# Masks ahead of a turn's gelus, paced weight rounding, the bounds check on ScalarE and interleaved first operands in a routing attention with an MLP

## The chip, the cores and the metric

The kernel runs on one core of a Trainium2 chip. The metric is the device time of one execution in microseconds (us). The engines of the core each work through an instruction stream of their own, in order: TensorE (PE in the profile, its weight loads PEld), VectorE (DVE), ScalarE (ACT), GpSimd (POOL), and SyncE (SP), which issues most of the DMAs. They wait for each other by semaphores.

## The reference

A masked attention, in which a query sees only the keys of its own cluster, is followed by an MLP with a quick gelu:

```python
# q, k, v: (B=4, H=8, S=768, D=64) float32; centroids: (8, 16, 64)
q_assign = argmax(q_n @ c_n)            # normalised vectors, 16 clusters
k_assign = argmax(k_n @ c_n)
mask = q_assign[:, :, :, None] == k_assign[:, :, None, :]
scores = where(mask, (q @ k.T) / 8, -1e9)
attn = exp(scores - max); attn /= attn.sum() + 1e-9
x = (attn @ v).transpose(0, 2, 1, 3).reshape(3072, 512)
h = x @ w_in                            # w_in (512, 2048), float64
g = h * (1 / (1 + exp(-1.702 * h)))
out = (g @ w_out).astype(float32)       # w_out (2048, 512), float64
```

Both MLP weights arrive as float64 and have to be brought to float32 on the chip.

## The kernel before

The 32 heads are handled as 16 pairs p of two heads each, and a pair as two groups g of 384 queries. A group consists of six units u, one for each 128 keys. Two units make a turn t, so there are 96 turns, 24 for each batch element. A half block is the 12 turns that give 384 rows of x for all eight heads.

**Attention.** For each unit `scores` runs the matmuls of both heads into a PSUM tile s (L344; there are two, each of two banks) and the exponential on ScalarE in place (L349). `mask` multiplies on VectorE by "query's code equals key's code" (L358, twice for each unit) and gives A; GpSimd adds the A of a group into sum (L368, five times for each group). `values` multiplies A by v on TensorE (L379) one turn later. `normalise` comes two turns after a group's last unit: a matmul with ones (L391), reciprocal (L394) and product (L396) on VectorE, and a bounds check there (L398) whose result is kept in sums. Its verdict is read near the end and would send the program to a general path.

**Preparing a pair.** `PREP` is a list of seven steps: four turns of q and k by transposes on TensorE (L254), each copied out of PSUM (L260 on ScalarE, L262 on VectorE for the first of the four); `prep_near` (L271, L277), the products with the centroids; `prep_assign` (L282 and five operations on VectorE from L288 on), the codes; `prep_spread` (L309, the conversion L314, and two DMAs L316, L318), which sends the queries' codes through DRAM to all partitions as qb. The wrapper `prep` also issues loads: v of the pair before step 0, and the next q or k behind steps 1 and 3. The pools of these loads have few buffers, so a load waits for what frees its buffer, and SP issues everything in order.

**Weights.** They come in 32 chunks of 512 KB. Rounding step i issues the load of chunk i + 2 (L145), splits chunk i (L158, L160 on VectorE, L162, L164 on ScalarE) and joins chunk i - 1 (L170, L173 on VectorE, product L176 on GpSimd). The tile raw has three buffers, the tile e two. The order of the chunks is w_in first; each four chunks serve four MLP chunks.

**MLP.** The half block's 28 chunks are queued by the normalise of its last group: 16 of `first` (L417, tanh L422 on ScalarE, gelu L424 on VectorE, which frees the PSUM bank) and 12 of `second` (L434, output L440, L441). In each turn the loop takes as many as are due, part ahead of the preparation steps and part at the end of the turn. They share three PSUM banks m with the preparation and with normalise.

**Order.** The schedule is written out by hand: the engines get their instructions in program order. One turn before is: scores, MLP chunks, preparation steps, rounding steps by

```python
round_to(int(t * 2 / 3 if t < TB / 2 else
             TB / 3 + (t - TB / 2) * 2.3) - 1)
```

then masks, values of the turn before, normalise, MLP chunks. TB is 24. `first` and `second` call round_to themselves, too, so that no chunk comes ahead of its weights.

Of the kernel before, what the change touches and what calls it, by code (L numbers as in the profile page):

```python
# [8 lines left out]
FP32 = mybir.dt.float32  # L9
BF16 = mybir.dt.bfloat16  # L10
I32 = mybir.dt.int32
# [27 lines left out]
def fast(  # L39
# [113 lines left out]
    def split_w(i):  # L153

        hi = w_raw[i][:, :, 1]
        w = w_chunks[i][0]
        e = wp.tile([P, WN], I32, name="e", bufs=2)
        nc.vector.tensor_scalar(out=e, in0=hi, scalar1=EXP, scalar2=None,  # L158
                                op0=ALU.bitwise_and)
        nc.vector.tensor_scalar(out=w.bitcast(I32), in0=hi, scalar1=0xFFFFF,  # L160
                                scalar2=None, op0=ALU.bitwise_and)
        nc.scalar.activation(out=e, in_=e, func=AF.Relu, scale=8.0,  # L162
                             bias=low[:, 0:1])
        nc.scalar.activation(out=w, in_=w.bitcast(I32), func=AF.Copy,  # L164
                             scale=2.0 ** -20, bias=1.0)
        w_pow[i] = e
# [12 lines left out]
    w_done = [0]  # L179

    def round_to(n):

        while w_done[0] <= min(n, NW):
            i = w_done[0]
            if i < NW:
                load_w(i + 2)
                split_w(i)
            if i:
                join_w(i - 1)
            w_done[0] += 1  # L190

# [19 lines left out]
                   allow_small_or_imprecise_dtypes=True)  # L211
    sums = const.tile([P, 2 * NPAIR], FP32, name="sums")

# [34 lines left out]
    def prep_turn(p, i):  # L248
# [9 lines left out]
        dst = T[p, w][:, h * HALF:(h + 1) * HALF]  # L258
        if h or w:
            nc.scalar.copy(dst, ps[:, 0:HALF])  # L260
        else:
            nc.vector.tensor_copy(out=dst, in_=ps[:, 0:HALF])  # L262

# [42 lines left out]
    def prep_spread(p):  # L306
# [6 lines left out]
        row = asg.tile([n, P], U8, name="row")  # L313
        nc.vector.tensor_copy(out=row, in_=ps[0:n, 0:P])  # L314
        line = dram.tile([n, P], U8, name="line")
# [70 lines left out]
    def normalise(g):  # L386
# [3 lines left out]
        for a in range(2):  # L390
# [6 lines left out]

        nc.vector.scalar_tensor_tensor(  # L398
            out=rec, in0=ps[:, 0:HALF], scalar=1.0, in1=rec, op0=ALU.mult,
            op1=ALU.max, accum_out=sums[:, g:g + 1])  # L400
        if g % HP == HP - 1:
# [54 lines left out]
    prep_at = {}  # L456
    for p in range(2, NPAIR):
        b, hp = divmod(p, HP)
        for i, step in enumerate(PREP):
            if b == 0:  # L460
                t = (hp - 2) * TG + i * TG // len(PREP)
            else:
                t = b * TB + (-20, -8, -2, 1)[hp] + i
            prep_at.setdefault(t, []).append((p, i))
# [12 lines left out]
    owed = 0.0  # L477
    for p in range(2):
        for i in range(len(PREP)):
            prep(p, i)  # L480
    for t in range(NT + 2):
        us = range(2 * t, 2 * t + 2) if t < NT else ()
        for u in us:
            scores(u)
        owed = owed + rate if ffn else 0.0
        n = min(int(owed), len(ffn))
# [3 lines left out]
        for p, i in prep_at.get(t, ()):  # L490
            prep(p, i)
        round_to(int(t * 2 / 3 if t < TB / 2 else
                     TB / 3 + (t - TB / 2) * 2.3) - 1)
        for u in us:
            mask(u)
        if 1 <= t <= NT:
            for u in range(2 * t - 2, 2 * t):
                values(u)
        if t >= 2 and (t - 2) % TG == TG - 1:
            normalise((t - 2) // TG)  # L500
        for _ in range(n // 2):
            ffn.popleft()()


    ok = const.tile([P, 2 * NPAIR], FP32, name="ok")
    nc.vector.tensor_scalar(out=ok, in0=sums, scalar1=LIMIT, scalar2=None,
                            op0=ALU.is_le)
    ok1 = const.tile([P, 1], FP32, name="ok1")
    nc.vector.tensor_reduce(out=ok1, in_=ok, axis=AX.X, op=ALU.min)
    ps = bank()  # L510
# [450 lines left out]
```

## Time and profile before

| | |
|---|---|
| median of 3 runs | 1183.4 us (1183.03 to 1183.71) |
| the profiled execution | 1185.81 us, span in the trace 1184.0 us |
| TensorE busy | 1090.9 us, 92% of the span |
| VectorE, GpSimd, ScalarE busy | 513.4, 334.5, 306.6 us |
| mean granted TensorE clock | 0.959 of full speed |
| bytes moved | 45.92 MB, 39 GB/s over the span |

The span is the time from the first to the last instruction in the trace. A share of busy time is a mean over stages that have different limits; the granted clock is that which the throttle allowed TensorE, full speed being 2.4 GHz and the level below it 1.2 GHz. In the names of the rows s, m, A, qb and so on are the tiles named above, and "<-" after the bracket's idle time names what ended it.

### The profile page before, as it was taken

To read this page: it belongs to the slowest core of one execution; us is meant where nothing else is said; L and a number is where in the kernel's file an instruction comes from. 1 tells how busy PE (TensorE), PEld (TensorE's weight loads), DVE (VectorE), ACT (ScalarE), POOL (GpSimd) and SP (SyncE) were. 2 spreads that over 40 slices of the span, in tenths; PEclk is the share of its full clock that TensorE was granted. 3 is DMA by queue.
4 is the path that set the end of the run, shared out by engine and by line. 5 is a ranking of instruction groups with operands and counts; after the bars stand their busy time and mean duration, and the time that the engine had idled before them with its cause. 6 is when DMAs were issued, how large, how long until landed. Compare 5 with 4: busy or idle time off the path is not lost. (4 is left out here: it accounts for less than half of the span.)

```text
span 1184.0 us, 10396 instructions
## 1 busy us (share of the span) xinstructions
PE 1090.9 (92%) x3842; PEld 495.7 (42%) x3842; DVE 513.4 (43%) x897; ACT 306.6 (26%) x505; POOL 334.5 (28%) x200
## 2 busy tenths in 40 slices
PE   5767767759999999999999999999999999999997
PEld 3322333323444444544445444544444434443553
DVE  3688564644355234443354225433355334441110
ACT  2434333331233113321233122321232122310110
POOL 0555433343133133323222223323233223330000
PEclk8887888878999999999999999999999999999999
DMA  7432232321111000001111000102000000000000
GB/s 184 121 87 60 75 99 84 101 73 45 43 47 34 9 16 23 14 14 52 49 37 31 9 25 14 27 1 65 10 8 7 9 19 1 1 9 18 1 9 20
DMA packets 65484, 45.92 MB, mean 39 GB/s; under 512 B 52112, under 2 KB 58256, under 8 KB 65424
## 3 DMA queue, kind: packets, MB, share of 16 engines
q1 hardware_dynamic: 65280, 45.12, 13.7%
q8 instruction: 33, 0.54, 0.2%
q14 instruction: 27, 0.22, 0.1%
q10 hardware_dynamic: 144, 0.03, 0.0%
HBM read 38.83 MB, written 6.32 MB: 38 GB/s over the span
## 5 line engine op out<-in xcount | busy, mean ns | idle before, releaser
L434 PE MATMUL m<-w_out,g 128*128 128x512 f32 x768 | 355.3, 610 | 14.9 <-POOL w_out L176 14.9
L417 PE MATMUL m<-x,w_in 128*128 128x384 f32 x1024 | 362.7, 503 | 1.4 <-DVE bad L515 1.2
L368 POOL TENSOR_TENSOR sum<-sum,A 128x768 f32<-128x768 f32 x128 | 231.6, 1810 | 356.6 <-DVE A L358 351.6
L358 DVE SCALAR_TENSOR_TENSOR A<-qb,code,s 128x384 f32<-128x384 uint8 x384 | 209.7, 607 | 132.7 <-ACT s L349 101.7
L417 PEld LDWEIGHTS m<-x,w_in 128*128 128x128 f32 x1024 | 190.4, 194 | 172.7 <-issue 42.1
L434 PEld LDWEIGHTS m<-w_out,g 128*128 128x128 f32 x768 | 141.1, 192 | 208.8 <-issue 182.3
L344 PE MATMUL s<-T,T 64*128 64x384 f32 x768 | 169.3, 554 | 49.5 <-DVE A L358 47.4
L349 ACT ACTIVATE s<-s 128x768 f32<-128x768 f32 x192 | 145.9, 794 | 239.8 <-PE s L344 239.8
L424 DVE SCALAR_TENSOR_TENSOR g<-g,m 128x384 f32<-128x384 f32 x128 | 70.8, 553 | 276.9 <-ACT g L422 276.9
L379 PE MATMUL o<-A,inv 128*64 128x384 f32 x768 | 150.6, 515 | 0.0
L422 ACT ACTIVATE g<-m 128x384 f32<-128x384 f32 x128 | 62.8, 491 | 307.7 <-PE m L417 307.7
L368 POOL TENSOR_TENSOR sum<-A 128x768 f32<-128x768 f32 x32 | 61.0, 1907 | 262.9 <-DVE A L358 188.8
L344 PEld LDWEIGHTS s<-T,T 64*128 64x128 f32 x768 | 70.3, 199 | 146.1 <-issue 99.0
L394 DVE RECIPROCAL short<-m 128x384 f32<-128x384 f32 x32 | 81.6, 2550 | 34.0 <-PE m L391 34.0
L379 PEld LDWEIGHTS o<-A,inv 128*64 128x64 f32 x768 | 47.9, 140 | 71.6 <-issue 69.9
L440 ACT ACTIVATE y<-m 128x512 f32<-128x512 f32 x24 | 14.3, 598 | 133.5 <-PE m L434 120.3
L260 ACT COPY T<-m 128x384 f32<-128x384 f32 x48 | 22.9, 479 | 56.8 <-PE m L254 56.1
L254 PE MATMUL m<-ident,in 128*128 128x128 f32 x192 | 35.7, 313 | 2.0 <-ACT T L260 1.1
L176 POOL TENSOR_TENSOR w_out<-w_out,e 128x512 f32<-128x512 f32 x16 | 20.6, 1289 | 58.2 <-DVE w_out L173 58.2
L162 ACT ACTIVATE e<-e,low 128x512 int32<-128x512 int32 x32 | 23.1, 721 | 49.1 <-DVE e L158 48.9
L288 DVE TENSOR_REDUCE best<-m 128x24 f32<-128x384 f32 x16 | 8.9, 555 | 61.6 <-PE m L282 61.6
L176 POOL TENSOR_TENSOR w_in<-w_in,e 128x512 f32<-128x512 f32 x16 | 20.3, 1267 | 53.8 <-DVE w_in L173 53.8
(56 smaller groups left out, 313.8 us busy)
## 6 DMA issues: line engine op xcount, KB each, us to landing
raw<-in_moe_w_in_dram SPq DMA_DIRECT2D x16, 512.0 KB, 4.0
raw<-in_moe_w_out_dram SPq DMA_DIRECT2D x16, 512.0 KB, 3.4
in<-in_q_dram SPq DMA_DIRECT2D x32, 192.0 KB, 3.9
in<-in_k_dram SPq DMA_DIRECT2D x32, 192.0 KB, 3.3
inv<-in_v_dram SPq DMA_DIRECT2D x16, 384.0 KB, 4.5
out_dram<-y SPq DMA_DIRECT2D x24, 256.0 KB, 2.0
qb<-line SPq DMA_DIRECT2D x16, 192.0 KB, 3.2
line<-row SPq DMA_DIRECT2D x16, 1.5 KB
```

What stands on the lines that cost most here:

```text
L176: nc.gpsimd.tensor_tensor(out=w, in0=w, in1=e.bitcast(FP32), op=ALU.mult)
L254: nc.tensor.transpose(out=ps[:, n * P:(n + 1) * P], in_=qk_in[p, w][:, h * NH + n].rearrange("p a d -> p (a d)"), identity=ident)
L344: nc.tensor.matmul(out=ps[:, a, 0:HALF], lhsT=T[p, 1][rows, kt * P:(kt + 1) * P], rhs=T[p, 0][rows, h * HALF:(h + 1) * HALF], start=True, ...
L349: nc.scalar.activation(out=s, in_=s, func=AF.Exp, scale=SCALE)
L358: nc.vector.scalar_tensor_tensor(out=A[:, a, :], in0=qcode[p][:, a, h * HALF:(h + 1) * HALF], scalar=code[p][:, kt % NH, 1, kt // NH, a:a ...
L368: nc.gpsimd.tensor_tensor(out=sum_of[g], in0=A_of[u - 1] if kt == 1 else sum_of[g], in1=A, op=ALU.add)
L379: nc.tensor.matmul(out=o_of[g][a * D:(a + 1) * D, 0:HALF], lhsT=v_in[p][:, a, kt, :], rhs=A[:, a, :], start=(kt == 0), stop=(kt == NJ - 1))
L394: nc.vector.reciprocal(out=rec, in_=ps[:, 0:HALF])
L417: nc.tensor.matmul(out=ps[:, 0:HALF], lhsT=w_in[:, c, f * P:(f + 1) * P], rhs=xT[c], start=(c == 0), stop=(c == NCH - 1))
L422: nc.scalar.activation(out=g, in_=ps[:, 0:HALF], func=AF.Tanh, scale=0.851)
L424: nc.vector.scalar_tensor_tensor(out=g, in0=g, scalar=1.0, in1=ps[:, 0:HALF], op0=ALU.add, op1=ALU.mult)
L434: nc.tensor.matmul(out=ps[:, 0:DM], lhsT=hs[f][:, n * P:(n + 1) * P], rhs=w_out[:, f, :], start=(f == 0), stop=(f == NF - 1))
```

## The change

Six edits go together.

1. The masks of a turn stand right behind its scores and one rounding step, ahead of the turn's first MLP chunks and preparation steps.
2. Rounding goes by the new `round_next`: one step in each turn, ahead of the masks, and from turn 12 on a second one behind normalise. round_to stays as a guard in the MLP chunks.
3. The tile e has three buffers.
4. The bounds check is two ScalarE copies that add up (L399): one of the sums of exponentials, one of their reciprocals. It leaves VectorE.
5. All copies of turned operands, and the conversion in prep_spread, are on ScalarE.
6. The second pair's four transposing steps stand ahead of the first pair's last step; its other three steps are in turns 0 and 1. The third and fourth pairs' steps go two to a turn, from turns 1 and 4 on.

The core of the diff:

```diff
-        e = wp.tile([P, WN], I32, name="e", bufs=2)
+        e = wp.tile([P, WN], I32, name="e")
...
+    def round_next():
+        i = w_done[0]
+        if i < NW:
+            load_w(i + 2)
+            split_w(i)
+        if 0 < i <= NW:
+            join_w(i - 1)
+        w_done[0] += 1
+
     def round_to(n):
-
         while w_done[0] <= min(n, NW):
-            i = w_done[0]
-            if i < NW:
-                load_w(i + 2)
-                split_w(i)
-            if i:
-                join_w(i - 1)
-            w_done[0] += 1
+            round_next()
...
-    sums = const.tile([P, 2 * NPAIR], FP32, name="sums")
+    sums = const.tile([P, 2, 2 * NPAIR], FP32, name="sums")
...
-        if h or w:
-            nc.scalar.copy(dst, ps[:, 0:HALF])
-        else:
-            nc.vector.tensor_copy(out=dst, in_=ps[:, 0:HALF])
+        nc.scalar.copy(dst, ps[:, 0:HALF])
...
-        nc.vector.tensor_copy(out=row, in_=ps[0:n, 0:P])
+        nc.scalar.copy(row, ps[0:n, 0:P])
...
-        nc.vector.scalar_tensor_tensor(
-            out=rec, in0=ps[:, 0:HALF], scalar=1.0, in1=rec, op0=ALU.mult,
-            op1=ALU.max, accum_out=sums[:, g:g + 1])
+        junk = short()
+        for i, t in enumerate((ps[:, 0:HALF], rec)):
+            nc.scalar.activation(out=junk, in_=t, func=AF.Copy,
+                                 accum_out=sums[:, i, g:g + 1])
...
-    for p in range(2, NPAIR):
+    for p in range(1, NPAIR):
         b, hp = divmod(p, HP)
-        for i, step in enumerate(PREP):
-            if b == 0:
-                t = (hp - 2) * TG + i * TG // len(PREP)
+        for i in range(4 if p == 1 else 0, len(PREP)):
+            if p == 1:
+                t = i - 4 - i // 6
+            elif b == 0:
+                t = (hp - 2) * TG + 1 + i // 2
             else:
                 t = b * TB + (-20, -8, -2, 1)[hp] + i
...
-    for p in range(2):
-        for i in range(len(PREP)):
-            prep(p, i)
+    for p, i in [(0, i) for i in range(6)] + [(1, i) for i in range(4)]:
+        prep(p, i)
+    prep(0, 6)
     for t in range(NT + 2):
         us = range(2 * t, 2 * t + 2) if t < NT else ()
         for u in us:
             scores(u)
+        round_next()
+        for u in us:
+            mask(u)
         owed = owed + rate if ffn else 0.0
...
         for p, i in prep_at.get(t, ()):
             prep(p, i)
-        round_to(int(t * 2 / 3 if t < TB / 2 else
-                     TB / 3 + (t - TB / 2) * 2.3) - 1)
-        for u in us:
-            mask(u)
         if 1 <= t <= NT:
             for u in range(2 * t - 2, 2 * t):
                 values(u)
         if t >= 2 and (t - 2) % TG == TG - 1:
             normalise((t - 2) // TG)
+        if t >= TB // 2:
+            round_next()
         for _ in range(n // 2):
             ffn.popleft()()
```

On VectorE in turn 14, the first with MLP chunks, before: a gelu of that turn, two rounding steps (L158, L160 split one chunk, L170, L173 join the chunk before it), the masks A, and the gelu of the turn's second chunk.

```order
L424 SCALAR_TENSOR_TENSOR g_866<-g_866,m_861 128x384
L158 TENSOR_SCALAR e_871<-raw_813 128x512
L160 TENSOR_SCALAR w_in_106<-raw_813 128x512
L170 SCALAR_TENSOR_TENSOR e_825<-raw_781,e_825 128x512
L173 SCALAR_TENSOR_TENSOR w_in_106<-raw_781,w_in_106 128x512
L158 TENSOR_SCALAR e_881<-raw_823 128x512
L160 TENSOR_SCALAR w_in_106<-raw_823 128x512
L170 SCALAR_TENSOR_TENSOR e_871<-raw_813,e_871 128x512
L173 SCALAR_TENSOR_TENSOR w_in_106<-raw_813,w_in_106 128x512
L358 SCALAR_TENSOR_TENSOR A_889<-qb_205,code_195,s_853 128x384 x2
L358 SCALAR_TENSOR_TENSOR A_893<-qb_205,code_195,s_857 128x384 x2
L424 SCALAR_TENSOR_TENSOR g_906<-g_906,m_901 128x384
```

The same place now, from the end of turn 14's masks to the start of turn 15's:

```order
L357 SCALAR_TENSOR_TENSOR A_943<-qb_235,code_195,s_925 128x384 x2
L424 SCALAR_TENSOR_TENSOR g_952<-g_952,m_947 128x384
L158 TENSOR_SCALAR e_961<-raw_911 128x512
L160 TENSOR_SCALAR w_out_107<-raw_911 128x512
L170 SCALAR_TENSOR_TENSOR e_931<-raw_879,e_931 128x512
L173 SCALAR_TENSOR_TENSOR w_out_107<-raw_879,w_out_107 128x512
L424 SCALAR_TENSOR_TENSOR g_974<-g_974,m_969 128x384
L158 TENSOR_SCALAR e_987<-raw_929 128x512
L160 TENSOR_SCALAR w_out_107<-raw_929 128x512
L170 SCALAR_TENSOR_TENSOR e_961<-raw_911,e_961 128x512
L173 SCALAR_TENSOR_TENSOR w_out_107<-raw_911,w_out_107 128x512
L357 SCALAR_TENSOR_TENSOR A_995<-qb_312,code_302,s_977 128x384 x2
```

Each gelu is now followed by one step, and the masks of turn 14 are ahead of both; those of turn 15 have one step and no gelu of their own turn ahead of them.

On TensorE at the start, before: behind the first pair's spread (L309) come the second pair's transposes (L254), near (L271), assignment (L282) and spread, and then the first scores (L344).

```order
L309 MATMUL m<-ident_h,qc 12x128
L254 MATMUL m<-ident,in 128x128 x12
L271 MATMUL m<-T_209,cT 32x384 x2
L271 MATMUL m<-T_223,cT 32x384 x2
L282 MATMUL m<-ident,short 128x128 x3
L309 LDWEIGHTS qc
L309 MATMUL m<-ident_h,qc 12x128
L344 MATMUL s<-T_151,T_165 128x384 x4
```

The same place now, where lines are one to two lower or higher by the edits (L281 is the first pair's assignment, L256 the transposes, L308 the spread, L343 the scores, L270 near):

```order
L281 MATMUL m<-ident,short 128x128 x3
L256 MATMUL m<-ident,in 128x128 x12
L308 LDWEIGHTS qc
L308 MATMUL m<-ident_h,qc 12x128
L343 MATMUL s<-T_151,T_165 128x384 x4
L270 MATMUL m<-T_201,cT 32x384 x2
L270 MATMUL m<-T_215,cT 32x384 x2
```

The second pair's transposes stand ahead of the first pair's spread, and its near matmuls behind the first scores instead of ahead of them.

On ScalarE in turn 16, where before no check stood, now two chunks' tanh, a copy of turned operands, the two check passes (L399, the second reads the reciprocal), the split's two operations, a tanh and the next turn's exponentials:

```order
L422 ACTIVATE g<-m 128x384 x2
L261 COPY T_1079<-m 128x384
L399 ACTIVATE short,sums<-m 128x384
L399 ACTIVATE short,sums<-short 128x384
L162 ACTIVATE e<-e,low 128x512
L164 ACTIVATE w_out<-w_out 128x512
L422 ACTIVATE g<-m 128x384
L348 ACTIVATE s<-s 128x2x384 x2
```

The check passes are ahead of the turn's last tanh and of the next turn's exponentials on this engine.

## Rows read from the trace of the kernel before

**Rows 1.** View: busy time of each engine by stage (PE, PEld, DVE, ACT, POOL), then PE clock, DMA share, GB/s.

```profile
23.46:123.53 100.07, 70.18 (x305) 28.29 (x305) 72.94 (x127) 40.76 (x64) 50.79 (x30) 0.81 0.35 94
123.53:316.26 192.73, 151.54 (x471) 66.19 (x471) 101.88 (x183) 58.80 (x97) 70.69 (x46) 0.87 0.26 75
449.05:578.74 129.69, 129.63 (x474) 59.68 (x472) 56.80 (x92) 31.98 (x53) 39.38 (x22) 1.00 0.10 27
449.05:531.30 82.25, 82.19 (x314) 39.49 (x312) 40.15 (x67) 22.87 (x39) 24.92 (x14) 1.00 0.06 15
```

**Rows 2.** View: who waited for whom, 123.53 to 316.26: us in total, times, longest.

```profile
PE s L344 <- DVE A L358: 30.9, 8, 6.2
...
PE m L434 <- POOL w_out L176: 14.9, 5, 3.4
```

**Rows 3.** View: order of time on VectorE in one turn: start, duration, line, idle before.

```profile
144.05 0.56 DVE L424 SCALAR_TENSOR_TENSOR g<-g,m 128x384 f32<-128x384 f32 x1 [5.30 <-ACT g L422]
...
147.87 0.43 DVE L158 TENSOR_SCALAR e<-raw 128x512 int32<-128x512 int32 x1 [1.38 <-POOL w_in L176]
...
149.75 2.18 DVE L358 SCALAR_TENSOR_TENSOR A<-qb,code,s 128x384 f32<-128x384 uint8 x4
```

**Rows 4.** View: order of time on TensorE, the next turn's scores.

```profile
151.03 2.70 PE L344 MATMUL s<-T,T 64*128 64x384 f32 x8 [3.31 <-DVE A L358]
```

**Rows 5.** View: order of time at the start, several engines.

```profile
15.01 0.27 PE L309 MATMUL m<-ident_h,qc 128*12 128x128 bf16 x1 [2.63 <-DVE qc L302]
...
16.91 0.35 SPq L318 DMA_DIRECT2D qb<-line  x1
...
23.46 2.93 PE L344 MATMUL s<-T,T 64*128 64x384 f32 x8
...
27.73 2.18 DVE L358 SCALAR_TENSOR_TENSOR A<-qb,code,s 128x384 f32<-128x384 uint8 x4
```

**Rows 6.** View: DMA issues of the first 30 us: KB each, median us to landing.

```profile
qb<-line SPq DMA_DIRECT2D x2, 192.0 KB, 4.2
...
raw<-in_moe_w_in_dram SPq DMA_DIRECT2D x2, 512.0 KB, 6.7
```

**Rows 7.** View: groups by line on VectorE, 23.46 to 123.53: busy, mean ns, idle before.

```profile
L394 DVE RECIPROCAL short<-m 128x384 f32<-128x384 f32 x3 | 7.7, 2555 | 1.7 <-PE m L391 1.7
...
L262 DVE COPY T<-m 128x384 f32<-128x384 f32 x3 | 1.7, 558 | 9.8 <-PE m L254 9.8
...
L288 DVE TENSOR_REDUCE best<-m 128x24 f32<-128x384 f32 x3 | 1.7, 556 | 6.2 <-PE m L282 6.2
...
L314 DVE CAST row<-m 12x128 uint8<-12x128 bf16 x4 | 1.1, 279 | 3.4 <-PE m L309 3.4
```

**Rows 8.** View: order of time on VectorE and GpSimd, 63 to 72 us.

```profile
63.30 0.40 DVE L158 TENSOR_SCALAR e<-raw 128x512 int32<-128x512 int32 x1
...
65.17 2.17 DVE L358 SCALAR_TENSOR_TENSOR A<-qb,code,s 128x384 f32<-128x384 uint8 x4
...
65.32 1.27 POOL L176 TENSOR_TENSOR w_in<-w_in,e 128x512 f32<-128x512 f32 x1 [6.06 <-DVE w_in L173]
...
66.55 3.76 POOL L368 TENSOR_TENSOR sum<-sum,A 128x768 f32<-128x768 f32 x2
...
67.27 1.37 DVE L158 TENSOR_SCALAR e<-raw 128x512 int32<-128x512 int32 x1
...
68.56 2.04 DVE L160 TENSOR_SCALAR w_in<-raw 128x512 int32<-128x512 int32 x1
...
71.72 2.18 DVE L358 SCALAR_TENSOR_TENSOR A<-qb,code,s 128x384 f32<-128x384 uint8 x4
```

**Rows 9.** View: groups by line, whole span: busy us, mean ns, idle before.

```profile
L260 ACT COPY T<-m 128x384 f32<-128x384 f32 x48 | 22.9, 479 | 56.8 <-PE m L254 56.1
...
L396 DVE TENSOR_TENSOR x<-x,short 128x384 f32<-128x384 f32 x32 | 22.0, 688 | 1.2
...
L398 DVE SCALAR_TENSOR_TENSOR short<-m,short 128x384 f32<-128x384 f32 x32 | 17.8, 557 | 1.1
```

More of the change, by code (lines that the diff above doesn't have):

```diff
@@ L500, in fast @@
             normalise((t - 2) // TG)
+        if t >= TB // 2:
+            round_next()
         for _ in range(n // 2):
             ffn.popleft()()
-    ok = const.tile([P, 2 * NPAIR], FP32, name="ok")
+    ok = const.tile([P, 2, 2 * NPAIR], FP32, name="ok")
     nc.vector.tensor_scalar(out=ok, in0=sums, scalar1=LIMIT, scalar2=None,
@@ L508, in fast @@
     ok1 = const.tile([P, 1], FP32, name="ok1")
-    nc.vector.tensor_reduce(out=ok1, in_=ok, axis=AX.X, op=ALU.min)
+    nc.vector.tensor_reduce(out=ok1, in_=ok, axis=AX.XY, op=ALU.min)
     ps = bank()
```

## The prediction

> **What bounds the kernel now.** I read the busy time by stages first. The cuts are starts of turns, and a turn start is the moment at which TensorE begins a turn's score matmuls. Counting those, turn 0 begins at 23.46, turn 14 at 123.53, turn 26 at 316.26, turn 38 at 449.05 and turn 50 at 578.74. The MLP chunks of a half block run in the twelve turns that start two turns after its attention: those of the first half block in turns 14 to 25.
>
> The reader is to see in [rows 1] that the same kind of work takes two very different times. Turns 38 to 49 take 129.7 us, TensorE is busy for 129.6 of them and its granted clock is 1.00. Turns 14 to 25 hold the same matmuls (24 turns is the period of the schedule) and take 192.7 us, with TensorE busy 151.5, its clock at 0.87 and VectorE busy 101.9. So 63.0 us are lost in turns 14 to 25, part as idle time and part as matmuls at the lower of the two clock levels after the idle. From turn 26 on nothing is to be had: TensorE is the bound. Turns 0 to 13 carry no MLP work; there VectorE is the busiest engine, 72.9 of 100.1 us.
>
> The waits of turns 14 to 25 say who holds TensorE up [rows 2]: 30.9 us in 8 waits of the score matmul for VectorE's masks (a score bank comes free only when its mask has read it), and 14.9 us for output weights that GpSimd has not yet joined. The order of time of one such turn shows why the masks are late. VectorE sits 5.30 us in front of a gelu, whose tanh is not there yet, and only after it come two rounding steps, with 1.38 us of waiting for GpSimd's product between them (the two-buffer tile e), and then the masks [rows 3]. The masks end, and TensorE starts the next scores 3.31 us after it had run out of work, the first of them at the slow level: 2.70 us [rows 4].
>
> **The change, part by part.**
>
> *Start.* Scores of turn 0 begin at 23.46 because TensorE turns the second pair, brings it through its assignment and waits for VectorE there; the first masks start at 27.73 [rows 5]. Afterwards the second pair's twelve transposes run while VectorE assigns the first pair, its later steps follow in turns 0 and 1. What is late next is the first pair's spread code. Now its matmul ran at 15.01, its broadcast was issued at 16.91 and took 4.2 us to land [rows 5, 6], so it was there at 21.1. In the new order that matmul stands behind the twelve transposes, its copy behind four copies on ScalarE (0.48 us each [rows 9]), and its DMAs on SP behind one load of v and two pairs of loads of k and q that wait for those transposes. I add 1 us: masks at 22.1 instead of 27.73, minus 5.6 us. Bounds: minus 6.6 without that delay, 0 if the second pair's operands arrive late (a landing of 6.7 us was seen in this stretch [rows 6]).
>
> *Turns 0 to 13.* VectorE is the engine that has to get through. A step there costs 1.87 us where GpSimd is quiet (63.30 to the masks at 65.17) and 4.45 where it follows the masks at once and runs into GpSimd's two sums (67.27 to 71.72) [rows 8]. In turns 0 to 13 the steps up to the last masks grow from ten to fifteen: 5 x 1.87 = 9.4. The second pair's assignment moves in: four operations like the reduction of 0.556 and a small one, 2.4. Away go three bounds checks (0.557 and a short read, 1.8), three copies (1.7) and four conversions (1.1) [rows 7, 9]. Collisions: now the pattern of [rows 8] occurs twice in the stage; afterwards a step stands directly in front of the masks of each turn, with nothing between it and the masks before in turns 2, 5, 8 and 11, where GpSimd has two sums to do: 2 more, 2 x 2.58 = 5.2. Together 72.9 + 12.4 = 85.3 busy. Idle time was 27.1 us; the 9.8 in front of the copies and 3.4 in front of the conversions [rows 7] go, as both leave VectorE, and so do waits behind the e buffer like that in [rows 3], some 3 us, since it gets a third one. I keep the other 11. That makes 96.3 us against 100.1, minus 3.7. Bounds: minus 14 with no idle time left; plus 24 if every step collides (11 x 2.58 more).
>
> The Trainium skill, page "SBUF — State Buffer", section "Who interferes with whom", says that VectorE and GpSimd share one port pair as an exclusive lock: whichever starts first holds it for its whole instruction and the other blocks. The trace agrees: 1.37 and 2.04 us beside running sums where 0.40 is the quiet time [rows 8]. By that rule, applied to all four VectorE instructions of a step, this change moves more steps beside sums, and the sum would be that of the second rival below, 1162 us.
>
> *Turns 14 to 25.* Masks now follow one rounding step and stand ahead of the turn's gelus, the second step stands behind the first gelus, and by turn 14 sixteen instead of ten steps are issued, so that input weights are complete before the first chunk and output weights one or more turns ahead of their use. What VectorE has to do in turns 14 to 21 (the last with two steps): eight times four masks 17.4, sixteen steps 29.9, sixteen gelus of 0.56 9.0, two normalisations (2.56 and 0.69) 6.5, one assignment 2.4: 65.2 us, against 82.25 us that TensorE needs for the same eight turns at full clock [rows 1]. Waits for GpSimd: 16 x 2.58 = 41 at most. I take two full collisions (the short turns with two sums) and a wait for one product of 1.27 in each turn, 15 us: 80 us, just under TensorE's time. So TensorE is the bound, with little room: at the start of turn 14 VectorE still has a normalisation and two steps (7 to 8 us) ahead of the masks, which costs TensorE about 2 us, and uneven turns about 3. I take 129.7 + 5 = 134.7 instead of 192.7, minus 58.0. Bounds: 129.7 (minus 63), and 152 if every step collides (106 of VectorE's time against 82).
>
> *Costed at nothing.* The bounds check on ScalarE: two passes like the copy of 0.48 for each of 32 groups, 31 us on an engine that is busy 32 of 129.7 us [rows 1, 9]. The second pass waits for the reciprocal of 2.56 us, and tanh and the next turn's exponentials queue behind it; the cover is that TensorE has a turn's scores and a chunk to do before it needs a bank of theirs. From turn 26 on order alone changes under a saturated TensorE. Each rounding step also moves its load on SP, two ScalarE operations and GpSimd's product; the loads are the third rival.
>
> **Sum.** -5.6 - 3.7 - 58.0 = -67.3. The profiled execution took 1185.8 (span 1184.0), 2.4 more than the median of the runs shown; the difference is applied to that median: 1183.4 - 67.3 = 1116.
>
> **Rivals.**
> (1) *Slower: ScalarE held by the reciprocal.* The place is the second check pass. If tanh and exponentials come so late behind it that TensorE stalls for a bank, each of the 28 groups from turn 14 on pays. It decides from 67.3 / 28 = 2.4 us of stall per group on. At 3.6 us it gives 1116 + 101 = 1217. Against it: the hold is a reciprocal and a pass, 3.0 us, and a chunk with the scores takes longer; for it, VectorE may reach the reciprocal late. 3 in 100.
> (2) *Every step collides with GpSimd.* Turns 0 to 13 grow by 28 us (11 more collisions) and turns 14 to 21 last VectorE's 106 us instead of TensorE's 82, 18 more than the 5 I allow: 1116 + 28 + 18 = 1162. For it: GpSimd's sums now follow the masks with a step coming right behind. Against it: most turns have an assignment, a normalisation or a gelu between. This is the page's lock taken to its end. 12 in 100.
> (3) *The loads of weights gate the steps.* A load waits until the join two steps earlier has freed its buffer, so two steps cannot be closer than landing, issue and one step, 6.7 + 1.9 + about 0.5 = 9 us [rows 6, 8], a little below TensorE's 10.3 us a turn. If other loads ahead of them on SP add 4 us, eight turns grow by some 2.5 us each: 1136. 8 in 100.
> (4) *No effect:* masks come free early but TensorE waits for weights at the same places as long as before: 1183. Against it: the steps are ahead by six at turn 14. 2 in 100.
>
> **How the numbers follow.** My forecast, TensorE bound from about turn 14 on, has 72 in 100 and spans 1100 to 1132 (start and first stage between their bounds without rival 2, turns 14 to 25 between 130 and 142). Below 1100 I leave 3. The range 1100 to 1146 takes in the forecast and rival 3, 80 in 100. A measurement of this kernel can tell about 0.2% from no change. Faster: 72 + 3 + 12 + 8 = 95. Same 2. Slower 3.
>
> **What would show it.** First masks near 22 us; turn 14 starts near 114; turns 14 to 25 last near 135 us with the clock at 0.97 or more; waits of scores for masks there fall from 30.9 to under 6 us and those for output weights to nothing. Long durations (over 1 us) of the two split operations, counted, decide between forecast and rival 2; idle time of VectorE in front of a split that ends with a DMA shows rival 3; ScalarE's waits in front of its check passes, with TensorE idle behind, rival 1. The prediction is wrong if turns 14 to 25 stay above 150 us, or if a turn after 26 gets longer.

## The result, and the profile after

The changed kernel takes 1124.42 us (median of 4 runs, 1121.11 to 1125.44) where the kernel before, run on the same chip, takes 1183.56 (4 runs, 1183.03 to 1184.95). The ratio taken over all runs, not over the medians, is 0.9494, with an interval of 0.9473 to 0.9515. The span of the profiled execution is 1122.7 us instead of 1184.0, 61.3 less. TensorE is busy 1066.9 us, 95% of it, at a mean granted clock of 0.978.

The busy time by stages, with cuts at the same turns as in [rows 1]: turns 0 to 13, then 14 to 25, 26 to 37 and 38 to 49. The last line is the part of the second stage up to turn 21, the last turn with two rounding steps.

```profile
16.49:122.53 106.04, 72.38 (x317) 29.19 (x317) 89.27 (x137) 51.76 (x96) 56.26 (x33) 0.77 0.44 120
122.53:259.94 137.41, 130.85 (x472) 59.56 (x472) 103.30 (x151) 57.70 (x110) 66.39 (x43) 1.00 0.29 87
259.94:391.51 131.57, 131.49 (x491) 60.07 (x490) 50.98 (x85) 38.72 (x75) 32.95 (x19) 1.00 0.10 28
391.51:521.20 129.69, 129.62 (x474) 59.66 (x472) 53.60 (x80) 38.27 (x76) 39.44 (x22) 1.00 0.10 27
122.53:212.50 89.97, 83.41 (x311) 39.37 (x311) 86.58 (x131) 45.62 (x86) 51.30 (x35) 1.00 0.36 107
```

The reader is to see two opposite things. Turns 14 to 25 fell from 192.7 to 137.4 us, TensorE is busy for 130.9 of them and its clock is 1.00. Turns 0 to 13 grew from 100.1 to 106.0, and VectorE's busy time there from 72.9 to 89.3. The last line says which engine sets the pace in turns 14 to 21: VectorE is busy for 86.6 of 90.0 us and TensorE for 83.4. All of TensorE's idle time in the stage, 6.6 us, lies there; from turn 22 on TensorE is the bound. In a table, by the moments that the prediction cuts at:

| part | before | after | difference | predicted |
|---|---|---|---|---|
| to the first masks | 27.73 | 24.48 | -3.3 | -5.6 |
| first masks to turn 14 | 95.80 | 98.05 | +2.3 | -3.7 |
| turns 14 to 25 | 192.73 | 137.41 | -55.3 | -58.0 |
| turn 26 to the end | 867.74 | 862.76 | -5.0 | 0 |
| span | 1184.0 | 1122.7 | -61.3 | -67.3 |

The waits of TensorE in turns 14 to 25, answering to [rows 2]: us in total, times, longest.

```profile
PE s L343 <- DVE A L357: 3.6, 3, 2.5
PE m L390 <- DVE g L424: 1.5, 1, 1.5
PE m L417 <- DVE x L395: 1.1, 1, 1.1
PE m L417 <- DVE g L424: 0.4, 1, 0.4
```

The scores' wait for the masks fell from 30.9 us to 3.6, and the wait for output weights (14.9) is gone. One of these turns in order of time, VectorE first, then TensorE; it answers to [rows 3] and [rows 4].

```profile
134.02 2.18 DVE L357 SCALAR_TENSOR_TENSOR A<-qb,code,s 128x384 f32<-128x384 uint8 x4
136.12 0.54 DVE L424 SCALAR_TENSOR_TENSOR g<-g,m 128x384 f32<-128x384 f32 x1
136.59 0.91 DVE L158 TENSOR_SCALAR e<-raw 128x512 int32<-128x512 int32 x1
137.42 2.03 DVE L160 TENSOR_SCALAR w_out<-raw 128x512 int32<-128x512 int32 x1
...
143.75 2.18 DVE L357 SCALAR_TENSOR_TENSOR A<-qb,code,s 128x384 f32<-128x384 uint8 x4
```

```profile
135.29 1.97 PE L343 MATMUL s<-T,T 64*128 64x384 f32 x8 [2.46 <-DVE A L357]
...
145.03 1.96 PE L343 MATMUL s<-T,T 64*128 64x384 f32 x8 [0.77 <-DVE A L357]
```

VectorE now goes from masks to gelu to step without a pause; the 5.30 us that it sat in front of a gelu in [rows 3] are not there. The scores wait 0.77 us, or 2.46 in turn 15 behind a long split, instead of 3.31, and take 1.97 us for eight matmuls instead of 2.70.

The groups by line on VectorE, first of turns 0 to 13, then of 14 to 25 (busy, mean ns, idle before):

```profile
L357 DVE SCALAR_TENSOR_TENSOR A<-qb,code,s 128x384 f32<-128x384 uint8 x55 | 30.0, 606 | 14.3 <-DMA qb<-line 9.1 <-ACT s L348 5.2
L160 DVE TENSOR_SCALAR w_in<-raw 128x512 int32<-128x512 int32 x14 | 13.9, 994 | 0.0
L158 DVE TENSOR_SCALAR e<-raw 128x512 int32<-128x512 int32 x14 | 9.6, 686 | 0.0
...
L292 DVE TENSOR_TENSOR short<-short,rank 128x384 f32<-128x384 f32 x4 | 6.0, 1489 | 0.1
```

```profile
L158 DVE TENSOR_SCALAR e<-raw 128x512 int32<-128x512 int32 x17 | 15.9, 934 | 0.0
L160 DVE TENSOR_SCALAR w_out<-raw 128x512 int32<-128x512 int32 x16 | 13.7, 854 | 0.0
```

A split operation takes 0.42 us where GpSimd is quiet. Here 9 of the 28 in turns 0 to 13 and 12 of the 34 in turns 14 to 25 took more than 1 us; before it was 4 of 20 and none of 44. Their surplus is 9.6 + 13.9 - 28 x 0.42 = 11.7 us in the first stage; the four L292 there (0.558 before) add 3.8.

The start, answering to [rows 5]: start, duration, and idle time before.

```profile
14.85 1.51 PE L256 MATMUL m<-ident,in 128*128 128x128 f32 x6 [1.47 <-DMA in<-in_k_dram]
...
16.29 0.27 PE L308 MATMUL m<-ident_h,qc 128*12 128x128 bf16 x1
16.39 1.23 SPq L110 DMA_DIRECT2D in<-in_q_dram  x2
...
17.67 0.65 SPq L315 DMA_DIRECT2D line<-row  x1
...
20.78 0.35 SPq L317 DMA_DIRECT2D qb<-line  x1
...
24.48 2.19 DVE L357 SCALAR_TENSOR_TENSOR A<-qb,code,s 128x384 f32<-128x384 uint8 x4 [9.13 <-DMA qb<-line]
```

Turn 0's scores start at 16.49, 7 us earlier, but the masks sit 9.13 us for the broadcast of the codes. It was issued 3.87 us later than in [rows 5]: 1.28 because the spread's matmul stands behind transposes that waited for k, 0.14 for the conversion on ScalarE, 0.63 because SP was issuing the next q loads, and 1.82 more for the small transfer ahead of it (3.11 us from its issue to that of the broadcast, 1.29 before).

Turn 1, TensorE and VectorE:

```profile
31.45 3.68 POOL L367 TENSOR_TENSOR sum<-sum,A 128x768 f32<-128x768 f32 x2
...
33.34 2.21 DVE L292 TENSOR_TENSOR short<-short,rank 128x384 f32<-128x384 f32 x1
...
36.40 0.27 PE L308 MATMUL m<-ident_h,qc 128*12 128x128 bf16 x1 [6.88 <-DVE qc L301]
...
40.83 2.21 PE L343 MATMUL s<-T,T 64*128 64x384 f32 x8
...
43.39 2.19 DVE L357 SCALAR_TENSOR_TENSOR A<-qb,code,s 128x384 f32<-128x384 uint8 x4 [5.18 <-ACT s L348]
```

The second pair's spread (L308) stands in the same turn as its assignment, so TensorE waits 6.88 us while VectorE finishes the masks and the assignment, one operation of which (L292) takes 2.21 us beside GpSimd's sum. The next scores start at 40.83, and now VectorE idles 5.18 us for them: the engine that should never be idle here.

### The profile page after: what moved, and what is told of

Its sections match the earlier page's. It is cut to its first block, busy times and chain, and to the rows that moved or that the text cites. A ratio compares the mean times of both kernels' runs of the same rounds, so it can differ in the third digit from the quotient of the medians.

```text
span 1122.7 us, 10374 instructions
## 1 busy us (share of the span) xinstructions
PE 1066.9 (95%) x3842; PEld 488.7 (44%) x3842; DVE 512.0 (46%) x801; ACT 346.2 (31%) x665; POOL 335.7 (30%) x200
## 5 line engine op out<-in xcount | busy, mean ns | idle before, releaser
L417 PE MATMUL m<-x,w_in 128*128 128x384 f32 x1024 | 355.9, 496 | 2.9 <-DVE bad L518 1.2
L434 PE MATMUL m<-w_out,g 128*128 128x512 f32 x768 | 348.7, 602 | 0.0
L417 PEld LDWEIGHTS m<-x,w_in 128*128 128x128 f32 x1024 | 186.6, 190 | 167.6 <-issue 37.6
L343 PE MATMUL s<-T,T 64*128 64x384 f32 x768 | 158.3, 528 | 20.3 <-DVE A L357 16.4
L343 PEld LDWEIGHTS s<-T,T 64*128 64x128 f32 x768 | 68.2, 193 | 112.8 <-issue 66.1
L399 ACT ACTIVATE short<-m 128x384 f32<-128x384 f32 x32 | 15.7, 491 | 150.5 <-DVE short L393 150.5
L261 ACT COPY T<-m 128x384 f32<-128x384 f32 x64 | 29.8, 477 | 50.2 <-PE m L256 50.2
L383 ACT COPY x<-o 128x384 f32<-128x384 f32 x32 | 15.3, 478 | 77.7 <-PE o L378 77.7
L256 PE MATMUL m<-ident,in 128*128 128x128 f32 x192 | 35.2, 309 | 3.2 <-DMA in<-in_k_dram 1.9
L256 PEld LDWEIGHTS m<-ident,in 128*128 128x128 f32 x192 | 25.3, 157 | 18.9 <-issue 10.2
```

Of the source, the lines that this page charges most:

```text
L256: nc.tensor.transpose(out=ps[:, n * P:(n + 1) * P], in_=qk_in[p, w][:, h * NH + n].rearrange("p a d -> p (a d)"), identity=ident)
L343: nc.tensor.matmul(out=ps[:, a, 0:HALF], lhsT=T[p, 1][rows, kt * P:(kt + 1) * P], rhs=T[p, 0][rows, h * HALF:(h + 1) * HALF], start=True, ...
L417: nc.tensor.matmul(out=ps[:, 0:HALF], lhsT=w_in[:, c, f * P:(f + 1) * P], rhs=xT[c], start=(c == 0), stop=(c == NCH - 1))
L434: nc.tensor.matmul(out=ps[:, 0:DM], lhsT=hs[f][:, n * P:(n + 1) * P], rhs=w_out[:, f, :], start=(f == 0), stop=(f == NF - 1))
```

## The experiments

The theory: turns 14 to 25 come back because the masks stand ahead of the gelus, with the rounding's spread for the weights beside it; the first stage fell short through the second pair's spread in turn 1 and through VectorE's collisions with GpSimd. The rivals: the spread alone does it, or the small edits (third e buffer, the check's place, the start) carry a part. Ratios are to the kernel before, run on the same chip each time. The stage times are read from each run's profile, so a sum of stages can differ from the difference of the medians by some us.

**The masks' place alone, in the kernel before** (b_masks):

```diff
             scores(u)
+        for u in us:
+            mask(u)
...
         round_to(int(t * 2 / 3 if t < TB / 2 else
                      TB / 3 + (t - TB / 2) * 2.3) - 1)
-        for u in us:
-            mask(u)
```

> The kernel before with one part of the change alone: the masks of a turn stand right behind its scores, and the rounding steps keep their old pace and place. My theory (the time comes from masks that no longer stand behind gelus and steps, and early weights are needed beside it): waits of scores for masks in turns 14 to 25 fall from 30.9 us to under 10, the waits for output weights stay near 15 us or grow, and turns 14 to 25 take 150 to 165 us instead of 192.7, so 1145 to 1158 us in all. The rival (the earlier pace of rounding brings nearly all): 1175 us or more.

Measured: 1171.45 us, 0.9890 (0.9867 to 0.9913); turns 14 to 25 last 183.0 us. TensorE's waits in them:

```profile
PE m L434 <- POOL w_out L176: 16.4, 6, 7.6
PE m L417 <- DVE x L396: 7.6, 1, 7.6
PE m L417 <- DVE short L398: 6.7, 1, 6.7
PE m L254 <- DVE short L398: 6.3, 1, 6.3
```

No row names the masks any more, but only 13 us are won: neither range holds the time, and it is nearer to the rival's. The steps still come in bursts, and what stands behind a burst on VectorE is late in place of the masks: normalise, whose product is the input x of the first MLP chunk (L396) and whose check holds a PSUM bank (L398). The weights are as late as before.

**The pace of rounding alone, in the kernel before** (b_round):

```diff
-        round_to(int(t * 2 / 3 if t < TB / 2 else
-                     TB / 3 + (t - TB / 2) * 2.3) - 1)
+        round_to(t if t < TB // 2 else 2 * t - TB // 2)
...
             normalise((t - 2) // TG)
+        if t >= TB // 2:
+            round_to(2 * t - TB // 2 + 1)
```

> The kernel before with the new pace of rounding alone: one step in each turn ahead of the masks, from turn 12 on a second one behind normalise; the masks stay behind gelus and preparation. My theory: one step less between gelu and masks saves some 3 us in each of the turns 14 to 22 and the weight waits go, but the masks still wait for a gelu, so scores wait 15 us or more for masks in turns 14 to 25; 1145 to 1160 us. The rival (pace): 1122 to 1135 us.

Measured: 1144.36 us, 0.9661 (0.9634 to 0.9688); turns 14 to 25 last 145.9 us, turns 0 to 13 105.3. TensorE's waits in turns 14 to 25:

```profile
PE s L344 <- DVE A L358: 7.9, 5, 3.2
PE m L434 <- POOL w_out L176: 3.0, 1, 3.0
```

With the masks still behind the gelus, their wait falls from 30.9 to 7.9 us: what made them late was mostly the burst of steps ahead of them, not the gelu. The spread alone gives 40 of the change's 60 us by the ratios: the theory's first part falls, the rival holds for two thirds. The time lies between the two ranges. This edit spreads the steps and also has six more of them done by turn 14; no run has the one without the other.

**The change with the masks put back behind gelus and preparation** (a_mask_back):

```diff
         round_next()
-        for u in us:
-            mask(u)
...
             prep(p, i)
+        for u in us:
+            mask(u)
```

> The changed kernel with its masks put back behind the first chunks' gelus and the preparation, all else kept. My theory: the waits of scores for masks come back, 15 to 30 us in turns 14 to 25, and some in turns 0 to 13 behind the assignments; 1140 to 1165 us. The rival (pace): within 0.5% of 1124 us.

Measured: 1131.24 us, 0.9561 (0.9535 to 0.9586). Turns 0 to 13 104.0, 14 to 25 140.1, 26 to 94 744.1 (741.6 after). With the spread in place the masks' move is worth 6.8 us by the medians, near the rival and far from the theory. The stages show less: 2.7 in turns 14 to 25 and 2.5 in the turns behind them, while it costs 2 in the first stage, together 3. Another 1.7 us of the profiled difference lie behind turn 95, in a part that goes with no edit (see the end of the next section).

**The change with the old pace** (a_pace):

```diff
-        round_next()
+        round_to(int(t * 2 / 3 if t < TB / 2 else
+                     TB / 3 + (t - TB / 2) * 2.3) - 1)
...
-        if t >= TB // 2:
-            round_next()
```

> The changed kernel with the old pace of rounding, all steps of a turn ahead of its masks, masks still ahead of gelus. My theory: turns 0 to 13 get shorter by 8 to 15 us (five steps fewer), turns 14 to 25 longer by 8 to 20 us (bursts of two or three steps ahead of masks, the last output weights late); 1118 to 1135 us in all. The rival (pace): 1150 us or more.

Measured: 1145.98 us, 0.9683 (0.9656 to 0.9710); turns 0 to 13 101.0, 14 to 25 160.5. The time lies between the two ranges. TensorE's longest waits there:

```profile
PE m L434 <- POOL w_out L176: 12.1, 3, 5.5
PE s L343 <- DVE A L357: 4.0, 2, 3.1
```

The spread is worth 21.6 us with all other edits in place: it costs 5 us in the first stage and gives 23 in the second. The weights are the largest part: 12.1 of the 21.7 us for which TensorE idles in turns 14 to 25.

**Masks ahead and the old bursts behind normalise, in the kernel before** (b_masks_late):

```diff
             scores(u)
+        for u in us:
+            mask(u)
...
-        round_to(int(t * 2 / 3 if t < TB / 2 else
-                     TB / 3 + (t - TB / 2) * 2.3) - 1)
-        for u in us:
-            mask(u)
...
             normalise((t - 2) // TG)
+        round_to(int(t * 2 / 3 if t < TB / 2 else
+                     TB / 3 + (t - TB / 2) * 2.3) - 1)
```

> The kernel before with masks ahead (as in b_masks) and the old pace of rounding moved behind normalise, to the end of the turn. In b_masks TensorE waited three times 6 to 8 us for PSUM banks that a normalisation on VectorE held, each with a burst of two or three steps ahead of it. Theory (a burst ahead of normalise holds a bank that the matmuls of the next chunk need): these waits go, those for output weights stay, turns 14 to 25 fall from 183 to 158 to 170 us; 1145 to 1160 us in all. The rival (VectorE has too much to do in these turns wherever the steps stand): turns 14 to 25 stay above 178 us, 1166 us or more.

Measured: 1162.32 us, 0.9816 (0.9799 to 0.9833); turns 14 to 25 177.3. The waits for L396 and L398 are gone; two for gelus' banks (4.3 and 3.5 us) come in their place, and the burst's place makes 9 us, by the profiles half of it in turns 0 to 13 and half behind them. The output weights stay late, 17.9 us in 6 waits. The time lies between the two ranges. Neither place of the bursts gives what the spread gives.

**The third e buffer taken away** (a_e2):

```diff
-        e = wp.tile([P, WN], I32, name="e")
+        e = wp.tile([P, WN], I32, name="e", bufs=2)
```

> The changed kernel with two buffers of the tile e instead of three. Theory, after the runs before (the even pace of rounding brings most): a step's e was used by a product at least one step earlier, and steps no longer come in bursts, so the third buffer is worth little: 1122 to 1128 us (ratio to before 0.948 to 0.953). The rival (the waits behind e, 22.4 us in the kernel before, were a main part): 1132 us or more.

Measured: 1125.63 us, 0.9494 (0.9480 to 0.9508), the same. VectorE's groups in turns 14 to 25 say why:

```profile
L158 DVE TENSOR_SCALAR e<-raw 128x512 int32<-128x512 int32 x17 | 10.7, 628 | 7.0 <-POOL w_out L176 5.6 <-POOL w_in L176 1.4
```

7.0 us of waiting for GpSimd's product come back, and the splits lose 7.3 us of busy time (L158 10.7 for 15.9, L160 11.6 for 13.7). With a third buffer VectorE does not wait for GpSimd in front of the split, it waits inside it. Turns 14 to 25 last 136.0 us here, 1.4 less than with three buffers, and turns 0 to 13 108.4, 2.3 more: there 2.9 us of waiting come back and the splits take as long as with three.

**The check back on VectorE** (a_check):

```diff
...
-        junk = short()
-        for i, t in enumerate((ps[:, 0:HALF], rec)):
-            nc.scalar.activation(out=junk, in_=t, func=AF.Copy,
-                                 accum_out=sums[:, i, g:g + 1])
+        nc.vector.scalar_tensor_tensor(
+            out=rec, in0=ps[:, 0:HALF], scalar=1.0, in1=rec, op0=ALU.mult,
+            op1=ALU.max, accum_out=sums[:, g:g + 1])
```

> The changed kernel with the bounds check back on VectorE. Theory: VectorE is the bound of turns 0 to 13 and close to it to turn 21, so seven checks of 0.6 us come back there, 2 to 4 us, and nothing later; 1125 to 1129 us. The rival (the passes on ScalarE that wait for the reciprocal cost TensorE time): faster than the changed kernel, 1117 to 1122 us.

Measured: 1126.27 us, 0.9494 (0.9479 to 0.9509), the same; turns 0 to 13 105.3, 14 to 25 138.0. VectorE has 1.8 and 2.5 us more to do in the two stages, and TensorE's waits in turns 14 to 25 are the same within 0.1 us, but for one of 1.0 instead of 0.4 us.

**The old start** (a_start): the prologue and the table of preparation of the kernel before, in the changed kernel.

```diff
...
-    for p, i in [(0, i) for i in range(6)] + [(1, i) for i in range(4)]:
-        prep(p, i)
-    prep(0, 6)
+    for p in range(2):
+        for i in range(len(PREP)):
+            prep(p, i)
```

> The changed kernel with the old start: both first pairs prepared whole ahead of the first scores, the third and fourth pair's steps at their old turns. Theory: the first masks come some 3 us later (27.7 us), but the second pair's codes are there before turn 1, whose wait of 6.9 us is gone, so the interleaved start as it is brings nothing: turn 14 starts at 119 to 124 us, 1120 to 1126 us in all. The rival (the earlier first masks are kept to the end): 1127 to 1131 us.

Measured: 1126.91 us, 0.9513 (0.9497 to 0.9530), so the new start is worth about 2 us; the intervals overlap, and the time lies between the two ranges. First masks come at 25.77 and turn 14 starts at 124.82 (24.48 and 122.53 after).

**Four of five sums left out** (a_nosum): GpSimd adds only one of the five further A of a group, so the sums are not the reference's.

```diff
-        if kt == 0:
+        if kt != 1:
             return
```

> The changed kernel with four of the five adds of a group's sum left out (GpSimd adds only the first two A; the sums are not the reference's). It takes away most of the collisions of rounding steps with GpSimd. Theory (VectorE's time is the bound of turns 0 to 13, so what it loses at the shared port is lost in the end): the two split operations return to 0.42 us each, turns 0 to 13 get shorter by 9 to 16 us, turns 14 to 25 by 2 to 6; 1103 to 1114 us. The rival (VectorE would have idled there for TensorE or ScalarE anyway): 1119 to 1125 us.

Measured: 1107.61 us, 0.9349 (0.9335 to 0.9363); turns 0 to 13 94.5 us, 14 to 25 131.0. VectorE's groups in turns 0 to 13:

```profile
L160 DVE TENSOR_SCALAR w_in<-raw 128x512 int32<-128x512 int32 x14 | 10.2, 730 | 0.0
...
L158 DVE TENSOR_SCALAR e<-raw 128x512 int32<-128x512 int32 x14 | 5.9, 422 | 0.0
L292 DVE TENSOR_TENSOR short<-short,rank 128x384 f32<-128x384 f32 x4 | 3.8, 941 | 0.1
```

By the ratios the sums beside VectorE cost the changed kernel 17 us, 11.5 in the first stage and 6.4 in the second. The splits return to 0.42 us only in part, beside GpSimd's products and the sums that are left (L160, 730 ns). The 17 us are not the price of the collisions alone: without the sums GpSimd's products and what normalise waits for also come earlier, and the collisions that are left are not in it. Turns 14 to 25 end 1.3 us above the 129.7 that TensorE needs.

**The second pair's spread a turn later** (a_both), and the first pair's spread ahead of the second pair's last two transposing steps:

```diff
-                t = i - 4 - i // 6
+                t = i - 4
...
-    for p, i in [(0, i) for i in range(6)] + [(1, i) for i in range(4)]:
+    for p, i in ([(0, i) for i in range(6)] + [(1, 0), (1, 1), (0, 6),
+                                               (1, 2), (1, 3)]):
         prep(p, i)
-    prep(0, 6)
```

> The changed kernel with two moves at its start: the first pair's spread ahead of the second pair's last two transposing steps, and the second pair's spread one turn later. Theory: the first masks come 2 us earlier (the wait for the late k of the second pair no longer stands ahead of the spread), and TensorE no longer waits 6.9 us for the second pair's codes in turn 1; VectorE being the bound, 4 to 8 us of it stay: 1116 to 1121 us. The rival (VectorE has a fixed amount to do there, so nothing is gained): 1122 to 1126 us.

Measured: 1117.77 us, 0.9428 (0.9413 to 0.9442), faster than both kernels. TensorE at turn 1, then the two stages:

```profile
24.67 2.93 PE L343 MATMUL s<-T,T 64*128 64x384 f32 x8 [4.59 <-DVE A L357]
...
30.88 1.56 PE L343 MATMUL s<-T,T 64*128 64x384 f32 x8
```

```profile
16.63:116.19 99.56, 69.51 (x317) 28.31 (x317) 88.75 (x137) 51.79 (x95) 56.66 (x33) 0.83 0.48 129
116.19:253.60 137.41, 132.24 (x472) 60.44 (x472) 103.20 (x151) 57.72 (x110) 66.42 (x43) 0.99 0.30 87
```

Turn 1 lasts 6.2 us instead of 15.1, the first masks come at 23.39 instead of 24.48, and VectorE's wait of 5.2 us for the scores of turn 2 is gone. So the first masks come 1.1 us earlier, and from there to turn 14 another 5.3 us are won. All of the gain lies ahead of turn 14; its busy time there (88.8) is that of the changed kernel.

**That version with step and masks behind the preparation in turns 0 to 11** (a_both_late):

```diff
-        round_next()
-        for u in us:
-            mask(u)
+        if t >= TB // 2:
+            round_next()
+            for u in us:
+                mask(u)
...
             prep(p, i)
+        if t < TB // 2:
+            round_next()
+            for u in us:
+                mask(u)
```

> a_both with step and masks behind the preparation in turns 0 to 11, ahead of it later. With its masks behind the preparation the changed kernel had turns 0 to 13 shorter by 2 us. Theory (that came from the second pair's assignment alone, which a_both has already taken out of the way): 1116 to 1122 us, no gain over a_both. The rival (assignments ahead of masks are the better order there): 1111 to 1115 us.

Measured: 1122.56 us, 0.9479 (0.9464 to 0.9495). Turns 0 to 13 take 105.2 us, with this wait on TensorE:

```profile
PE s L343 <- DVE A L357: 32.6, 11, 4.5
```

With the wait of turn 1 gone, step and masks ahead are worth it in the first stage too (99.6); the edit moves both, and no run moves the masks alone here. Turns 14 to 25 take 134.9 us, 2.5 less than in a_both, so part of the gain is given back.

**That version with the second step only from turn 14 on** (a_both_14):

```diff
-        if t >= TB // 2:
+        if t >= TB // 2 + 2:
             round_next()
```

> a_both with the second rounding step of a turn from turn 14 on instead of 12, two steps fewer in turns 12 and 13. Theory (VectorE bounds turns 0 to 13 and TensorE turns 14 to 25, so a step is dearer in the first): turns 0 to 13 shorter by 3 to 6 us, turns 14 to 25 longer by 1 to 5 us because the last output weights come just in time; 1113 to 1119 us. The rival (turns 14 to 22 have no room for two more steps on VectorE): 1121 us or more.

Measured: 1121.78 us, 0.9477 (0.9458 to 0.9496); turns 0 to 13 98.5, 14 to 25 141.1, with

```profile
PE m L434 <- POOL w_out L176: 7.0, 2, 5.8
```

The rival's range holds the time. Two steps fewer ahead of turn 14 win 1 us there and 5.4 in turns 14 to 16, but the last output weights come late: turn 22 lasts 20.7 us instead of 11.5. The lead is needed at the end of the rounding, not at its start.

## Why the prediction was right, and where its terms were off

**Turns 14 to 25: right in mechanism and nearly in size** (-55.3 for -58.0). TensorE's clock is 1.00, for the 0.97 or more of the prediction, its waits for masks are 3.6 us, it has none for weights, and 6.6 us of idle time stand beside the 5 that the prediction allowed. "TensorE is the bound, with little room" holds only from turn 22 on. For turns 14 to 21 the prediction gave VectorE 80 us, just under TensorE's 82.25; VectorE was busy 86.6 of their 90.0 us and set the pace. Part of the 86.6 is the normalisation and the step that were left over from turn 13, which the prediction named and priced by themselves. In a_nosum, where VectorE has less to do, the whole stage takes 131.0. Its 15 us for GpSimd met the size by luck: they were 5 of collisions and 10 of waits for products, and the trace has 15.7 us of longer splits (15.9 + 13.7 + 0.4 - 34 x 0.42) and no wait. What the prediction left undecided the runs decide, against the theory of the experiments: the spread of the rounding carries most (40 us alone, 18 to 22 on top of the rest, by profiles and by medians), the masks' place 13 alone and 3 to 7 on top. The prediction read [rows 2, 3] as masks late behind a gelu and two steps; the steps were the larger part (b_round).

**The start: -3.3 for -5.6.** The added microsecond for a late spread was too small. The broadcast was issued at 20.78, not near 18, by the parts above. The prediction had named the late operands and SP's order, and its bounds hold the result; the small transfer's price it took from a quieter moment. From its issue to that of the broadcast the queues moved 5 GB/s before and 145 GB/s now.

**Turns 0 to 13: +2.3 for -3.7, the mis-sized term.** The larger part is in the sum itself, which takes the time ahead of the first masks away twice. The start term moves the first masks from 27.73 to 22.1. The stage term, 96.3 against 100.1, counts from turn 0's scores at 23.46, and the 9.8 us in front of copies that it takes away [rows 7] include the wait in this row of the kernel before, which ends ahead of the first masks:

```profile
27.25 0.56 DVE L262 COPY T<-m 128x384 f32<-128x384 f32 x1 [3.41 <-PE m L254]
```

This wait, this copy and one conversion fill the 4.3 us from 23.46 to 27.73, and the term takes all three away. So the prediction's 85.3 us of work and 11 of idle time lie behind the first masks, where the kernel before took 95.8: the term is +0.5, not -3.7, turn 14 starts near 118 and the sum is -63.1, or 1120 us. Turn 14 started at 122.53.

Behind the first masks the work came out as 89.3 us for 85.3 and the idle time as 8.8 for 11. The work is the collisions: four full ones were counted (4 x 2.58 = 10.3 us), the surplus was 11.7 + 3.8 = 15.5, since the L292 of each assignment collides as well. In the idle time two misses meet: the 6.2 us in front of the assignments (L288 in [rows 7]), which the prediction kept, went to nothing, and 5.2 us for the scores of turn 2, behind the second pair's spread, are new. The prediction did not count that spread's wait, and a_both, where it stands a turn later, loses it: 92.8 us from the first masks to turn 14, with 4.1 of them idle.

**Rival 2, collisions, is partly true:** 21 long splits instead of the 4 before, and 17 us less without most of the sums (a_nosum), but not to the end that gave 1162: in turns 14 to 25 the surplus is the 15.7 us above, of 41 at most. That a gelu, an assignment or a normalisation between masks and step kept it down, as the prediction argues, no run shows. **Rival 3, the loads,** did not occur: no idle time of VectorE in front of a split in the changed kernel. **Rival 1, ScalarE held by the reciprocal,** has its wait but not its price. One check on ScalarE, then TensorE beside it:

```profile
294.31 0.49 ACT L399 ACTIVATE short<-m 128x384 f32<-128x384 f32 x1 [4.21 <-DVE short L393]
294.70 0.19 ACT L399 ACTIVATION_READ_ACCUMULATOR short<-m 128x1 f32 x1
294.93 0.52 ACT L399 ACTIVATE short<-short 128x384 f32<-128x384 f32 x1
...
295.45 0.47 ACT L422 ACTIVATE g<-m 128x384 f32<-128x384 f32 x1
```

```profile
291.60 2.85 PE L417 MATMUL m<-x,w_in 128*128 128x384 f32 x8
294.38 1.56 PE L343 MATMUL s<-T,T 64*128 64x384 f32 x8
295.87 1.56 PE L417 MATMUL m<-x,w_in 128*128 128x384 f32 x4
```

ScalarE sits 4.21 us and the tanh behind it is late, but TensorE goes on through chunk, scores and chunk without a gap, and a_check, without the wait, takes the same time, 741.6 us from turn 26 to 94 in both.

**From turn 26 on: -5.0 for 0.** "Order alone changes under a saturated TensorE" overlooked small gaps: turns 28, 31, 52, 55, 76, 78 and 79 are 0.3 to 0.9 us shorter, no turn longer. In a_mask_back all of them are longer than after by 0.3 to 0.4, so the masks' place gives 2.5 us of the 3.5 up to turn 95; the rest lies in turns 28 and 52, where before TensorE waited for copies of turned operands, 1.1 us in 2 waits. The last 1.5 us belong to no edit and are luck: from the start of turn 95 to the end the profiles show either 121.0 to 121.2 us (the changed kernel, b_masks, a_pace, a_both) or 122.7 to 122.8 (the kernel before, b_round, a_e2, a_check), with masks ahead or not.

## What to carry to other kernels

When work that must be done by a deadline is put between others' work on an engine, spread it evenly and finish it a turn or more ahead; moving the victim ahead of a burst only hands the stall to whatever stands behind the burst next. When a step is moved earlier, look at what it waits for in its new turn (here a spread beside its own assignment): in a_both a turn later was worth some 5 us. When a sum has one term for a start and one for the stage behind it, let the second begin where the first ends. A gap that is taken out of one engine's queue can return as a longer instruction, so compare busy time plus idle time, not idle time alone.

## What the runs showed of the hardware

- The splits that had waited 7.0 us for GpSimd's buffer took 7.3 us longer when the buffer was free: in turns 14 to 25 VectorE's time beside GpSimd was lost either way. The operation L292, whose two inputs both lie in SBUF, is held too, 0.56 us quiet and 1.20 to 2.21 beside a sum. The Trainium skill, page "SBUF — State Buffer", section "Who interferes with whom", says so of an instruction with two SBUF inputs; the trace agrees.
- Both check passes wait for the reciprocal, also the first, which only reads the same PSUM tile: it starts at 294.31, at the end of a reciprocal from 291.72, and in all 32 groups 0.03 to 0.09 us behind the reciprocal's end. The prediction expected that of the second alone. The Trainium skill, page "PSUM — Partial Sum Buffer", section "PSUM bank collisions raise a hardware error", tells that the compiler's scheduler adds a dependency between instructions on different engines that touch the same part of a bank, for reads too; this trace agrees, though it does not show what put the wait there.
- ScalarE reads its accumulator in an instruction of its own, 0.19 us each (64 in the kernel, 12.2 us); VectorE's took 0.08.
- A transfer of 1.5 KB at the start took 3.11 us from its issue to that of the transfer that waits for it, where the queues moved 145 GB/s meanwhile, 3.58 where they moved 183 (a_both), and 1.29 where they moved 5 (before). That the traffic is the cause is argued, not shown.
